# One weight, two transfers: 16 partitions first, then 112

## The chip, the cores and the metric

The kernel runs on one core of one Trainium2 chip. The time is device microseconds of one execution; the number given for a kernel is the median of several. A profile is one further execution with the hardware profiler on; its times count from the start of its span.

## The reference

One decode step of a transformer block with adaptive layer norm, four sequences, width 512, everything in fp32:

```python
mod = (silu(c) @ w_mod).reshape(4, 6, 1, -1)            # c 4x512, w_mod 512x3072
sa, ca, ga, sb, cb, gb = (mod[:, i] for i in range(6))
h = layernorm(x) * (1 + ca) + sa
q = (h @ wq).reshape(4, 1, 32, 128).transpose(0, 2, 1, 3)   # wq 512x4096
p = softmax(q @ k_cache^T * 128**-0.5)                  # k_cache 4x32x4096x128
x = x + ga * ((p @ v_cache) merged over heads @ wo)     # v_cache as k_cache, wo 4096x512
h = layernorm(x) * (1 + cb) + sb
x = x + gb * (silu(h @ w1) @ w2)                        # w1 512x1792, w2 1792x512
```

The two caches are 268 MB each; everything else together is some 30 MB. With one query per sequence each cache element is used once.

## The kernel before, in words

The kernel is first recorded as a list of operations (the class Flow), with each operation's reads and writes by region. Flow works out from these which operation must wait for which, gives every transfer that someone waits for a semaphore of its own, and then emits the operations engine by engine in recorded order. All transfers are issued from SP (nc.sync), in one queue, in the order of the text.

SBUF holds three large slots of 64 KB per partition (ring, slots 0 to 2). Attention runs over 32 blocks n, each of four heads of one sequence: load_k and load_v (both through L374) bring one 8.4 MB block of K or V, 64 KB to each of 128 partitions. VectorE and GpSimd multiply K by the query (L568, GpSimd 40 of the 128 rows of a partition and VectorE 88), VectorE sums (L573), ScalarE takes the exponential (L587), and TensorE multiplies by V (L604). A block's load waits until the slot's former content has been used; K blocks alternate between slots 1 and 2, V blocks use slot 0 (the last one slot 1).

Before the blocks stands the front, which the change touches. Slot 0 holds the modulation weight w_mod there: 128 partitions with four of its rows each, which are one contiguous run of 48 KB per partition (wmv, wmt). Behind it in slot 0 lie the small tensors cg and x0, into which the condition c and the input x go as 16 rows of 512 bytes, to every eighth partition (SB = 8). Slot 2 holds the query weight wq, 64 KB per partition. SP issues, in this order: w_mod (L403), c (L404), x (L405), wq (L408), the first K block (L374). While these arrive, the vector and GpSimd engines build small constant masks. Then silu(c) is taken on ScalarE and VectorE (L466, L467), transposed (L470), multiplied by w_mod on TensorE (L483, sixteen products of it for the first two of the six modulations, 32 for the other four), spread (L491, L495) and copied out (L497); the first layer norm follows, and the query product with wq (L532, L540, then L559 and L563 for each block's query). The second K block goes into slot 2 and the first V block into slot 0, so each waits for the products that read wq or w_mod and the small tensors.

Behind the blocks come the output weight wo in four pieces and w1 and w2 in six (fetch, L366), the output projection (L650), the second layer norm, the feed-forward products (L725, L737), and the store of 16 rows of 512 bytes (L743).

Of the kernel before, what the change touches and what calls it, by code (L numbers as in the profile page):

```python
# [273 lines left out]
def adaln_attention_ffn_kernel(  # L274
# [12 lines left out]
    P = 128  # L287
# [94 lines left out]
    wmv = wm.rearrange("(p k) n -> p k n", p=P)  # L382
# [7 lines left out]
    wmt = s0.take(NK, 6 * D)  # L390
# [9 lines left out]
    xg = const.tile([P, P], F32, name="xg")  # L400
    nc.vector.memset(cg, 0.0)
    nc.gpsimd.memset(x0, 0.0)
    nc.sync.dma_start(wmt, wmv)  # L403
    nc.sync.dma_start(cg[::SB], c)  # L404
    nc.sync.dma_start(x0[::SB], x)  # L405
    s1 = Slot(2)
# [365 lines left out]
```

## Time and profile before

| what | value |
|---|---|
| median of 3 runs | 1316.1 us (1316.02 to 1316.14) |
| the profiled execution's own time | 1316.18 us |
| its span, first to last instruction | 1314.8 us |
| mean granted TensorE clock | 0.647 |
| read from HBM | 567.30 MB |
| busy: VectorE / GpSimd / TensorE / ScalarE | 975.6 / 393.6 / 367.4 / 64.7 us |

How to read the lines that follow: a row of the timeline is start, duration, engine, line of the kernel, operation, what is written and read, the count, and in brackets how long the engine stood idle before and what ended that. PEld is TensorE's weight load, SPq the queue of SP from which transfers are issued. A row of the transfers is target and source, the issuing queue, the count, the size, and the microseconds from issue to landing. A row of the stretches is from:to and length, the busy time of each engine with its number of instructions, the granted TensorE clock, the share of 16 DMA engines in use, and GB/s.

### The profile page before, as it was taken

Reading aid. Unit: us, or ns where it says so; the run is one execution under the profiler, and the core shown is the slowest. Engines: PE = TensorE matmul, PEld = TensorE weight load, DVE = VectorE, ACT = ScalarE, POOL = GpSimd, SP = SyncE. Lnnn points to the kernel's source line nnn. Section 1 sums busy time; section 2 is a strip of 40 time slices with the busy share of each in tenths; the row PEclk is TensorE's granted clock in tenths of the full one; section 3 lists DMA queues with packets and bytes.
Section 4 is the critical chain, followed back from the end, with each engine's and each line's share of the span. In section 5 each row is a group of like instructions: output and inputs, shape, how many; then the busy total and the mean of one; then the engine's idle time right before and its main releaser. Section 6 shows DMA issues by size and latency. Waiting matters only on the chain.

```text
span 1314.8 us, 6115 instructions
## 1 busy us (share of the span) xinstructions
PE 367.4 (28%) x2590; PEld 114.2 (9%) x2590; DVE 975.6 (74%) x256; ACT 64.7 (5%) x198; POOL 393.6 (30%) x106
## 2 busy tenths in 40 slices
PE   3302233211332321133232123323112332311257
PEld 1100101000010100001010000101000010000112
DVE  2399777977777887777788777779777778977762
ACT  1100000000000000000000000000000000000001
POOL 0244312333321333332133333123333212333300
PEclk9756666656666655666665566665566666556669
DMA  9999999999999999999999999999999999999998
GB/s 415 437 423 447 419 441 439 427 441 423 441 439 427 441 433 431 445 421 443 435 429 443 423 441 437 427 441 431 433 443 423 441 435 429 445 423 441 437 423 360
DMA packets 11050, 567.42 MB, mean 432 GB/s; under 512 B 1264, under 2 KB 1312, under 8 KB 1824
## 3 DMA queue, kind: packets, MB, share of 16 engines
q1 hardware_dynamic: 11040, 567.31, 99.7%
q8 instruction: 4, 0.07, 0.0%
q14 instruction: 6, 0.05, 0.0%
HBM read 567.30 MB, written 0.01 MB: 431 GB/s over the span
## 4 chain that ended last, share of the span: by engine, by line
DMA 60%; DVE 38%; PE 1%; another core or an unknown queue 1%; SPq 0%; issue 0%; ACT 0%; DVEq 0%; ACTq 0%
DMA slot<-in_A_k_cache_dram 54%; DVE sc L573 22%; DVE slot L568 15%; DMA slot<-in_B_w_dram 3%; DMA slot<-in_A_wq_dram 3%; PE q L532 1%; PE po L737 0%; DVE rm L577 0%; PE q L540 0%; SPq L366 0%; DVE tr L581 0%; SPq L405 0%; PE q L559 0%; ACT o L557 0%
## 5 line engine op out<-in xcount | busy, mean ns | idle before, releaser
L568 DVE TENSOR_TENSOR slot<-slot,q 128x11264 f32<-128x11264 f32 x32 | 380.4, 11887 | 259.8 <-DMA slot<-in_A_k_cache_dram 259.8
L573 DVE TENSOR_REDUCE sc<-slot 128x88 f32<-128x11264 f32 x64 | 552.9, 8680 | 1.1
L604 PE MATMUL po<-slot,pz 128*32 128x512 f32 x2048 | 294.6, 740 | 901.7 <-PEq L260 836.9
L568 POOL TENSOR_TENSOR slot<-slot,qw 128x5120 f32<-128x5120 f32 x32 | 353.5, 11046 | 220.7 <-DMA slot<-in_A_k_cache_dram 220.7
L589 POOL TENSOR_TENSOR pz<-sc,hm 128x256 f32<-128x256 f32 x64 | 38.1, 617 | 637.9 <-ACT sc L587 637.9
L604 PEld LDWEIGHTS po<-slot,pz 128*32 128x32 f32 x2048 | 80.8, 133 | 1096.6 <-issue 1088.7
L563 ACT ACTIVATE qw<-q 128x128 f32<-128x128 f32 x32 | 8.9, 278 | 562.7 <-DMA slot<-in_A_v_cache_dram 403.4
L557 ACT ACTIVATE o<-qn,sel 128x128 f32<-128x128 f32 x32 | 11.1, 394 | 377.3 <-DMA slot<-in_A_v_cache_dram 377.2
L617 PE MATMUL od<-pc,sg 128*64 128x128 f32 x128 | 17.0, 276 | 12.8 <-PEq L260 12.8
L639 DVE TENSOR_TENSOR o<-og,ra 128x512 f32<-128x512 f32 x2 | 1.4, 692 | 21.2 <-ACT og L620 21.2
L614 ACT ACTIVATE pc<-po 128x512 f32<-128x512 f32 x16 | 9.6, 597 | 151.7 <-PE po L604 151.7
L587 ACT ACTIVATE sc<-sc,nm 128x128 f32<-128x128 f32 x32 | 12.8, 399 | 72.9 <-DVE nm L583 72.6
L617 PEld LDWEIGHTS od<-pc,sg 128*64 128x64 f32 x128 | 13.5, 136 | 26.8 <-issue 26.8
L483 PE MATMUL q<-slot 128*32 128x512 f32 x48 | 9.0, 676 | 19.4 <-DVE slot L470 19.4
L559 PE MATMUL q<-o,blk 128*128 128x256 f32 x32 | 11.2, 431 | 1.5 <-ACT o L557 1.5
L467 DVE SCALAR_TENSOR_TENSOR slot<-slot 128x128 f32<-128x128 f32 x1 | 0.3, 292 | 13.6 <-ACT slot L466 13.6
L491 DVE TENSOR_TENSOR slot<-q,hm 64x256 f32<-64x256 f32 (+1 forms) x8 | 4.1, 548 | 8.2 <-PE q L483 7.3
L577 DVE TENSOR_REDUCE rm<-sc 128x1 f32<-128x128 f32 x32 | 9.1, 286 | 1.1
L650 PE MATMUL acc<-slot,oo 128*4 128x512 f32 x64 | 8.9, 709 | 3.3 <-DVE oo L642 2.5
L620 ACT ACTIVATE og<-od 32x128 f32<-32x128 f32 x32 | 8.5, 267 | 24.3 <-PE od L617 24.1
L549 DVE COPY qn<-q 32x128 f32<-32x128 f32 x2 | 0.6, 284 | 11.1 <-PE q L540 11.0
L581 DVE STREAM_TRANSPOSE tr<-rm 128x32 f32<-128x32 f32 x32 | 6.8, 212 | 1.1
(85 smaller groups left out, 90.8 us busy)
## 6 DMA issues: line engine op xcount, KB each, us to landing
slot<-in_w_mod_dram SPq DMA_DIRECT2D x1, 6144.0 KB, 17.2
slot<-in_A_wo_dram SPq DMA_DIRECT2D x1, 4096.0 KB, 22.2
slot<-in_B_w_dram SPq DMA_DIRECT2D x1, 2688.0 KB, 34.1
slot<-in_A_wo_dram SPq DMA_DIRECT2D x1, 2304.0 KB, 25.2
slot<-in_A_wo_dram SPq DMA_DIRECT2D x1, 1536.0 KB, 27.9
slot<-in_B_w_dram SPq DMA_DIRECT2D x1, 1536.0 KB, 39.0
slot<-in_B_w_dram SPq DMA_DIRECT2D x1, 1280.0 KB, 41.5
slot<-in_B_w_dram SPq DMA_DIRECT2D x1, 896.0 KB, 35.8
```

The costliest lines, as they stand in the source:

```text
L483: nc.tensor.matmul(p[W * u : W * (u + 1), :], csT[:, k, :], wmt[:, k, (i + u) * D : (i + u + 1) * D], start=k == 0, stop=k == NK - 1,)
L532: nc.tensor.matmul(pq[i][W * g : W * (g + 1), :], hT[:, k, :], wqt[:, k, ch * CW : (ch + 1) * CW], start=k == 0, stop=k == NK - 1,)
L557: nc.scalar.activation(m[:, b, :], qn, AF.Copy, scale=sel[:, n + b : n + b + 1])
L559: nc.tensor.matmul(p, blk.rearrange("p i x -> p (i x)"), m, start=True, stop=True)
L568: eng.tensor_mul(kt[n][:, lo:hi, :], kt[n][:, lo:hi, :], src[n].unsqueeze(1).to_broadcast([P, hi - lo, Dh]))
L573: nc.vector.tensor_reduce(sc[n][:, lo:hi], kt[n][:, lo:hi, :], axis=AX.X, op=ALU.add)
L577: nc.vector.tensor_reduce(nm[n], sc[n], axis=AX.X, op=ALU.min)
L587: nc.scalar.activation(sc[n], sc[n], AF.Exp, bias=nm[n], scale=-1.0, accum_out=rs[i][:, c : c + 1])
L589: nc.gpsimd.tensor_mul(pz[h][:, : HG * W].rearrange("p (g x) -> p g x", g=HG)[:, :, E:].rearrange("p g (i j) -> p g i j", i=HP), sc[n][:, ...
L604: nc.tensor.matmul(po[u][W * g : W * (g + 1), :], pz[h][:, o : o + W], vt[n][:, JJ * j : JJ * (j + 1), :].rearrange("p j d -> p (j d)"), s ...
L614: nc.scalar.activation(m, po[u].rearrange("p (j d) -> p j d", j=JJ), AF.Copy)
L617: nc.tensor.matmul(p[: 2 * W], sg[:, j, :], m[:, j, :], start=j == 0, stop=j == JJ - 1)
```

## The change

The load of the modulation weight is issued as two transfers in place of one: partitions 0 to 15 (P // 8 = 16), then partitions 16 to 127. Both write the same places as before, from the same places in memory, 48 KB contiguous per partition: 0.79 MB and 5.51 MB. Each has a semaphore of its own, and the first product that reads the weight waits for both. The order of all other transfers stays.

```diff
     nc.vector.memset(cg, 0.0)
     nc.gpsimd.memset(x0, 0.0)
-    nc.sync.dma_start(wmt, wmv)
+    for lo, hi in ((0, P // 8), (P // 8, P)):
+        nc.sync.dma_start(wmt[lo:hi], wmv[lo:hi])
     nc.sync.dma_start(cg[::SB], c)
     nc.sync.dma_start(x0[::SB], x)
     s1 = Slot(2)
```

## The prediction

> **What bounds the kernel now.** I read the head of the page and its third part first, because they say at once whether any engine has room.
>
> ```profile
> span 1314.8 us, 6115 instructions
> PE 367.4 (28%) x2590; PEld 114.2 (9%) x2590; DVE 975.6 (74%) x256; ACT 64.7 (5%) x198; POOL 393.6 (30%) x106
> DMA packets 11050, 567.42 MB, mean 432 GB/s; under 512 B 1264, under 2 KB 1312, under 8 KB 1824
> q1 hardware_dynamic: 11040, 567.31, 99.7%
> DMA 60%; DVE 38%; PE 1%; another core or an unknown queue 1%; SPq 0%; issue 0%; ACT 0%; DVEq 0%; ACTq 0%
> ```
>
> No computing engine is busy for more than 74% of the span, but the packets of the one load queue fill 99.7% of what 16 DMA engines have. The last line, the chain that ended last, gives VectorE 38%. That share misleads: the chain steps through VectorE where a buffer is handed back, while the transfers run on. Whether they do run on is a question for the stretches of the span.
>
> ```profile
> core 0: us, PE busy (x) PEld busy (x) DVE busy (x) ACT busy (x) POOL busy (x), PEclk, DMA share, GB/s
> 0.00:2.00 2.00, 0.00 (x0) 0.00 (x0) 0.66 (x5) 1.26 (x1) 1.40 (x9) 1.00 0.68 197
> 2.00:18.00 16.00, 0.00 (x0) 0.00 (x0) 2.81 (x14) 0.02 (x1) 0.40 (x1) 1.00 1.02 435
> 18.00:37.30 19.30, 14.84 (x68) 3.94 (x68) 6.73 (x18) 3.08 (x9) 0.29 (x1) 1.00 1.00 435
> 37.30:58.10 20.80, 9.69 (x70) 2.94 (x70) 1.05 (x3) 2.70 (x7) 0.00 (x0) 0.81 0.95 410
> 58.10:1310.00 1251.90, 340.54 (x2388) 105.80 (x2388) 963.77 (x215) 57.67 (x181) 391.53 (x96) 0.63 1.00 434
> 1310.00:1314.80 4.80, 2.33 (x64) 1.56 (x64) 0.58 (x2) 0.00 (x0) 0.00 (x0) 1.00 0.09 35
> ```
>
> The next to last column is the DMA share (a packet counts in the stretch where it starts, hence 1.02). From 2 us to 1310 us it is 1.00 but for 0.95 in one stretch of 20.8 us, that is about 1.0 us not used. There is no idle time of the transfers in which a delay could disappear, and none that an earlier start would fall into. So the time is one stream of bytes with a head of some 2 us and a tail of under 5 us: what the weight's transfer loses or wins at the front arrives at the end.
>
> Last, the front itself: issues in order of time, and the time from issue to landing.
>
> ```profile
> 0.74 0.39 SPq L403 DMA_DIRECT2D slot<-in_w_mod_dram  x1
> 1.19 0.60 SPq L404 DMA_DIRECT2D slot<-in_c_dram  x1
> 1.83 0.83 SPq L405 DMA_DIRECT2D slot<-in_A_x_dram  x1
> 2.70 0.58 SPq L408 DMA_DIRECT2D slot<-in_A_wq_dram  x1
> 18.16 0.31 ACT L466 ACTIVATE slot<-slot 128x128 f32<-128x128 f32 x1 [16.14 <-DMA slot<-in_c_dram]
> 19.38 5.40 PE L483 MATMUL q<-slot 128*32 128x512 f32 x16 [19.38 <-DVE slot L470]
> 36.45 0.79 ACT L497 ACTIVATE mod<-q 128x128 f32<-128x128 f32 x4 [7.03 <-PE q L495]
> 37.33 7.08 PE L532 MATMUL q<-slot 128*32 128x512 f32 x64 [0.92 <-DMA slot<-in_A_wq_dram]
> ```
>
> ```profile
> slot<-in_w_mod_dram SPq DMA_DIRECT2D x1, 6144.0 KB, 17.2
> slot<-in_c_dram SPq DMA_DIRECT2D x1, 8.0 KB, 17.0
> out_dram<-slot SPq DMA_DIRECT2D x1, 8.0 KB, 1.7
> ```
>
> The weight lands at 0.74 + 17.2 = 17.94 us, the condition c right behind it (18.16 us), and the query weight at 37.3 us, back to back.
>
> **How a transfer is laid on the 16 engines.** All transfers are issued from SP; their number is needed, and these rows and those above give it.
>
> ```profile
> slot<-in_A_k_cache_dram SPq DMA_DIRECT2D x32, 48.0
> slot<-in_A_v_cache_dram SPq DMA_DIRECT2D x32, 29.2
> 1262.77 4.22 SPq L366 DMA_DIRECT2D slot<-in_A_wo_dram  x4
> 1267.03 15.07 SPq L366 DMA_DIRECT2D slot<-in_B_w_dram  x6
> ```
>
> 64 + 4 + 6 and the five single ones (weight, c, x, query weight, output) are 79. The page counts 1264 packets under 512 B, and 1264 = 79 x 16: one closing packet for each engine and transfer. So the three transfers of 16 rows also ended on 16 engines each. From 512 B to 2 KB there are 1312 - 1264 = 48 packets, 3 x 16 rows of 512 B: a row travels whole, as one packet. The change therefore very likely does what its words say: 16 rows of 48 KB, one per engine, then 7 per engine, where before it was 8 per engine.
>
> One row of 48 KB (49,152 B) takes an engine 0.997 x 16 x 1314.8 us x 49,152 / 567.31 MB = **1.82 us**. Eight are 14.54 us.
>
> **The change part by part.**
>
> *The head.* The slowest engine landed at 17.94 us, so its eight rows began in effect at 17.94 - 14.54 = 3.40 us, 2.66 us after the issue. The output, 16 rows of 512 B, has landed everywhere 1.7 us after its issue. A first transfer of 16 rows can thus have all engines moving by 0.74 + 1.7 = 2.44 us: a gain of at most 0.96 us, at least nothing (the first rows may be slow for another reason than the number of rows announced). I take 0.96, since the output is the only row here of a 16-row transfer with nothing ahead of it.
>
> *The issue.* One more issue on SP costs 0.39 to 0.60 us there by the rows at L403 and L404. Behind it stand the issues of c, x, the query weight and the first K block; each comes that much later and none is missed, because their packets queue behind 14.5 us of rows anyway. The second part is issued some 0.45 us after the first, before any engine is through its 1.82 us row. The extra 16 closing packets are below what this view resolves. Cost: nothing; without that cover, 0.6 us.
>
> *The wait.* The first product (L483) waits for one transfer more. PE is held there until 19.38 us by VectorE's transpose of silu(c), and c is queued behind both parts of the weight, so the new wait ends first. Nothing else stands behind it on PE but the modulation products themselves.
>
> *The rows.* This is the term that decides. In every large transfer of this trace the 16 engines serve 128 rows, and they run at 434 GB/s for 1250 us, never in each other's way. 16 streams that never meet, on 128 partitions, mean that if the way into the memory is narrow, there are 16 ways of 8 partitions each and each engine keeps to its own. The first part of the change writes only partitions 0 to 15, all 16 engines at once. With g of its rows in one way it takes g x 1.82 us. No transfer here shows g (the 16 rows of c and x lie 8 partitions apart and are tiny). The bounds: g = 1, the engine itself is the limit or neighbours never share, and the change costs nothing here; g = 8, a way is a block of 8 neighbours. Between 2 and 8 I take the geometric middle, **g = 4**: 4 x 1.82 = 7.27 us for 0.79 MB that cost 1.82 us before.
>
> While this lasts the other ways stand idle, and each still has 8 rows to come. The second part is then not 7 but at least 8 x 1.82 = 14.54 us. So for any g above 1 the loss is the whole first part: g x 1.82 us. If the 7 rows of an engine straddle two ways, engines meet now and then in the second part as well: between nothing and one row (1.82 us) more. I take half, 0.91.
>
> [...]
>
> *Sum.* -0.96 (head) + 7.27 (first part, after which the second takes as long as the whole did) + 0.91 = **+7.2 us**. On the profiled execution's own 1316.18 us (span 1314.8 and 1.4 around it; the median of the runs is 1316.1, the same to 0.1) that gives **1323.4 us**.
>
> *Does it arrive at the end?* c, the query weight and the first K block queue behind the weight and slide as it does. If the modulation chain slid further than the query weight (they end within 0.1 us of each other, 37.24 and 37.3), the next cover is the first K block:
>
> ```profile
> 48.51 0.28 ACT L563 ACTIVATE qw<-q 128x128 f32<-128x128 f32 x1 [0.79 <-PE q L559]
> 58.13 11.89 DVE L568 TENSOR_TENSOR slot<-slot,q 128x11264 f32<-128x11264 f32 x1 [10.61 <-DMA slot<-in_A_k_cache_dram]
> 46.34 0.33 SPq L374 DMA_DIRECT2D slot<-in_A_v_cache_dram  x1
> 1310.04 2.33 PE L737 MATMUL po<-slot 128*32 128x128 f32 x64 [0.84 <-DMA slot<-in_B_w_dram]
> ```
>
> The query is ready at 48.8 us and its K block comes at 58.1, 9.3 us of cover; the V block that reuses this slot is issued at 46.3, nearly 12 us ahead of need. The last row shows the end waiting for the last weight's transfer, so a late stream is a late end.
>
> **The rivals.**
>
> *Engines don't meet (g = 1).* Against my forecast: each engine's rate, 27 GB/s, may be the engine's own limit and not that of a way, and the trace would look exactly as it does. Then only the head counts: 0 to -0.96 us, **1315.2 to 1316.2 us**, not slower. It decides if the first 16 rows are in within about 1.82 + 0.96 + 2.6 = 5.4 us of movement.
>
> *Another width.* With g = 2 the sum is 3.63 - 0.96, **1318.9 us**; with g = 8 it is 14.54 - 0.96, **1329.8 us**. Same signs in the trace, other sizes.
>
> *Rounds of neighbours.* If the second part also deals 16 neighbouring partitions at a time, all eight rounds cost 7.27 us: 58.2 - 14.5 = +43.6, **about 1359 us**. Against it: the 128-row loads run undisturbed, so their dealing isn't of this kind.
>
> *The delay is absorbed.* Something would have to make up 5 us in the stream; the rows show 1.0 us unused. **Within 2 us of 1316.1.**
>
> **How the numbers follow.** Forecast (g = 4) 0.68; g = 2 0.06; g = 8 0.06; engines don't meet 0.15; rounds 0.03; absorbed 0.02. The range runs from 1318.8 (g = 2) to 1329.8 (g = 8), which holds 0.80 and leaves out the last three. A difference under 0.2% (2.6 us) can't be told from none here. Slower: 0.68 + 0.06 + 0.06 + 0.03 = 0.83. Same: 0.14 of the case without meeting, and the absorbed one, 0.16. Faster: 0.01, if the head gives far more than its bound.
>
> **What would show it.** The DMA rate between about 2.4 and 9.7 us near 108 GB/s instead of 435, the second part landing near 25 us instead of 17.94, c right behind it, the query weight near 44.5 and the first K block near 65; from there all rows shifted alike, the DMA share 1.00 and the durations of the instructions unchanged. If the weight still lands by 18 us, the step on the rows is wrong and the time is 1316. If it lands at 25 us and the end doesn't move, the reading of the stream is wrong.

## The result

The changed kernel takes **1331.1 us** (median of 4 runs, 1330.95 to 1331.81) against 1316.1: a ratio of 1.0114 (95% interval 1.0102 to 1.0126), or 15.0 us more. Slower was forecast, but by 7.2 us, and the time lies above the range. The head of the page, its third part and the transfer rows of the changed kernel, and the two issues of the weight as the timeline has them in one row:

```profile
span 1329.7 us, 6116 instructions
DMA packets 11066, 567.42 MB, mean 427 GB/s; under 512 B 1280, under 2 KB 1328, under 8 KB 1840
q1 hardware_dynamic: 11056, 567.31, 99.7%
slot<-in_w_mod_dram SPq DMA_DIRECT2D x1, 5376.0 KB, 32.7
slot<-in_w_mod_dram SPq DMA_DIRECT2D x1, 768.0 KB, 10.1
slot<-in_c_dram SPq DMA_DIRECT2D x1, 8.0 KB, 32.5
0.73 0.86 SPq L404 DMA_DIRECT2D slot<-in_w_mod_dram  x2
```

There are 16 packets more, all of them under 512 B: one closing packet per engine for one more transfer, and not one row more. The change is carried out as its words say. The queue is as "busy" as before, 99.7%, for 15 us longer: a share of busy time doesn't show that packets have become slow. The first issue begins at 0.73 us and the second some 0.45 us later (together they take 0.86 us), so the first part lands at about 10.8 us and the second at about 33.9 us. Before, the whole weight had landed at 17.94 us.

The stretches of the changed kernel, then its instructions in order of time:

```profile
0.00:2.00 2.00, 0.00 (x0) 0.00 (x0) 0.66 (x5) 1.27 (x1) 1.40 (x9) 1.00 2.03 270
2.00:9.40 7.40, 0.00 (x0) 0.00 (x0) 2.81 (x14) 0.01 (x1) 0.40 (x1) 1.00 0.85 139
9.40:34.00 24.60, 0.00 (x0) 0.00 (x0) 0.00 (x0) 0.00 (x0) 0.00 (x0) 1.00 0.92 235
34.00:53.10 19.10, 15.58 (x68) 4.01 (x68) 6.73 (x18) 2.30 (x5) 0.29 (x1) 1.00 1.01 439
53.10:73.10 20.00, 9.69 (x70) 2.94 (x70) 1.05 (x3) 3.49 (x11) 0.00 (x0) 0.86 0.98 424
73.10:1325.00 1251.90, 339.98 (x2392) 105.67 (x2396) 963.76 (x215) 57.52 (x181) 391.47 (x96) 0.63 1.00 434
```

```profile
34.13 0.31 ACT L467 ACTIVATE slot<-slot 128x128 f32<-128x128 f32 x1 [32.12 <-DMA slot<-in_c_dram]
35.31 6.13 PE L484 MATMUL q<-slot 128*32 128x512 f32 x16 [35.31 <-DVE slot L471]
53.26 7.07 PE L533 MATMUL q<-slot 128*32 128x512 f32 x64 [0.19 <-DMA slot<-in_A_wq_dram]
73.16 11.89 DVE L569 TENSOR_TENSOR slot<-slot,q 128x11264 f32<-128x11264 f32 x1 [9.71 <-DMA slot<-in_A_k_cache_dram]
```

Everything happened in the first 34 us. While the weight arrives, the core moves 139 and then 235 GB/s in place of 435 (a packet counts in the stretch where it starts, so 11 of the first part's 16 rows stand in the stretch from 0 to 2 us); from 34 us on it is at full rate again, and the 1251.9 us of the blocks move at 434 GB/s, as before. silu(c) starts 15.97 us later than before (34.13 against 18.16), the query product 15.93 (53.26 against 37.33), the first K block's product 15.03 (73.16 against 58.13), and the end comes 14.9 later. About 0.9 us came back in the stretch of the first K block, which used 0.95 of the engines before and uses 0.98 now; why was not tried. All else arrived at the end, as the stream has no slack.

The first part, 0.79 MB, behaves much as forecast: by the packet records of the trace its 16 rows run from 1.78 to 9.01 us, 7.23 us where 7.27 were expected. The second, 5.5 MB, lands 23 us after the first, where at least 14.5 and most likely 15.4 were expected.

### The profile page after: what moved, and what is told of

Same layout as the page of the kernel before. It is cut to its first block, busy times and chain, and to the rows that moved or that the text cites. A ratio compares the mean times of both kernels' runs of the same rounds, so it can differ in the third digit from the quotient of the medians.

```text
span 1329.7 us, 6116 instructions
## 1 busy us (share of the span) xinstructions
PE 367.4 (28%) x2590; PEld 114.1 (9%) x2590; DVE 975.6 (73%) x256; ACT 64.6 (5%) x198; POOL 393.6 (30%) x106
## 3 DMA queue, kind: packets, MB, share of 16 engines
q1 hardware_dynamic: 11056, 567.31, 99.7%
## 4 chain that ended last, share of the span: by engine, by line
DMA 59%; DVE 38%; PE 2%; another core or an unknown queue 1%; issue 0%; ACT 0%; SPq 0%; POOL 0%; DVEq 0%; ACTq 0%; POOLq 0%
DMA slot<-in_A_k_cache_dram 53%; DVE sc L574 22%; DVE slot L569 15%; DMA slot<-in_B_w_dram 3%; DMA slot<-in_c_dram 2%; PE q L484 1%; PE q L533 1%; PE q L496 0%; PE po L738 0%; DVE slot L492 0%; DVE rm L578 0%; PE q L541 0%; DVE tr L582 0%; SPq L366 0%
```

## The experiments

Most runs leave the weight's transfer as it was and put one extra transfer of 48 KB rows ahead of it. It goes into the slot of the first K block, where nobody reads it and the K block later overwrites it, so all computation is that of the kernel before. Since the stream of transfers sets the time, what such a transfer costs is seen in the time of the kernel. The K block's issue then waits until the extra transfer has landed (27.5 us in the run with 112 rows, where it is 3.3 before); the query weight ahead of it lands only at 61.2 us there, so the stream doesn't run dry. The three runs with 16 rows read the same rows of memory, and so do the five with 64, so what differs between them is where they write. The edit, of which only the target differs from run to run:

```diff
+    probe = Slot(1).take(NK, 6 * D)
+    nc.sync.dma_start(probe[TARGET], wmv[:ROWS])
     nc.sync.dma_start(wmt, wmv)
```

Two readings stand against each other. By the prediction's the place decides: g rows in one way take g x 1.82 us. By theory **N** any transfer with fewer than 128 rows is slow, wherever it writes. And where engines meet, either each loses only where it meets another itself, or all 16 go at the pace of those that meet; the trace of before doesn't tell which.

**Sixteen rows, three spacings.** Targets 32:93:4, 0:121:8 and 0:16.

> The kernel before, with one extra transfer ahead of the modulation weight: 16 rows of 48 KB into the slot that the first K block takes later, to partitions 32, 36, ... 92, every fourth. Nobody reads them. [...] Theory N (any transfer with fewer than 128 rows is slow, wherever it writes): +7.2 us, as the first part of the change is said to have cost.

> The same extra transfer to partitions 0, 8, ... 120, every eighth. [...] Theory N: +7.2 us.

> The same extra transfer to partitions 0 to 15, as the first part of the change has it. [...] Theory N: +7.2 us. If only the second part of the change were slow, +1.8 us.

Measured: 1318.4 us (+2.3), 1319.8 us (+3.7; median of eight, of which one took 1334.8) and 1323.0 us (+6.9, ratio 1.0052, 1.0035 to 1.0068), beside 1316.1 before. The landing of the extra transfer in the same order, one row from each kernel's list of transfers:

```profile
slot<-in_w_mod_dram SPq DMA_DIRECT2D x1, 768.0 KB, 4.9
```

```profile
slot<-in_w_mod_dram SPq DMA_DIRECT2D x1, 768.0 KB, 6.7
```

```profile
slot<-in_w_mod_dram SPq DMA_DIRECT2D x1, 768.0 KB, 10.0
```

The same bytes: 1.8 us more to every eighth partition than to every fourth of 32 to 92, and 5.1 us more to the block of 0 to 15. That is once and nearly three times 1.82 us, the time of one row; N, by which all three cost the same, falls. The rest to three times is in the start: by the packet records the spread rows begin at 2.12 us in both kernels and the block at 1.76, so from its first packet the block takes 5.46 us more than the first transfer, 3 x 1.82. Four row times, the forecast's guess, is what the block of 16 shows. And the spread rows cost 2.3 us, not the 0.9 that one row time less the forecast's gain at the head (1.82 - 0.96) gives. Of the 0.5 us over their row time, 0.35 us is that later start (2.12 against 1.77 before); the block doesn't have it. A gain at the head from announcing 16 rows first is not to be seen in either.

**The 112 rows alone.** Target 16:128.

> The kernel before, with an extra transfer of 112 rows of 48 KB to partitions 16 to 127 of the slot of the first K block, ahead of the whole modulation weight: the second part of the change without the first. [...] Engines never in each other's way: 7 x 1.82 = +12.7 us. The second part slow only because the first had set the engines out of step: +12.7 to +14.5 us.

Measured: 1338.4 us, **+22.3** (ratio 1.0168, 1.0151 to 1.0185). The second part is slow by itself; no first part is needed to set the engines out of step. With the 16 rows' 6.9 it also gives the change: 6.9 + 22.3 - 14.5 (the 128 rows that are no longer there) = 14.7, measured 15.0. The 22.3 us lie 9.6 us above seven rows of 1.82 us (12.7).

**Two transfers, cut the other way.**

```diff
-    nc.sync.dma_start(wmt, wmv)
+    fetch(wmt, wmv, 0, 1, NK)
```

Here fetch issues one transfer for the first of a partition's four rows of the weight and one for the other three.

> The weight in two transfers as in the change, but cut along the contiguous run and not along the partitions: all 128 partitions with 12 KB each, then all 128 with 36 KB each. [...] If two transfers in place of one are what costs: +15 us.

Measured: 1316.4 us, ratio 1.0001 (0.9991 to 1.0011). Two transfers in place of one cost nothing that can be told, if both go to all 128 partitions.

**Sixty-four rows, in the middle and below.** Targets 32:96 and 0:64.

> The kernel before, with an extra transfer of 64 rows of 48 KB to partitions 32 to 95 of the slot of the first K block, ahead of the modulation weight. [...] If a transfer with fewer than 128 rows were slow for its number of rows: +14.5 us. If neighbouring rows were dealt to neighbouring engines: 4 x 7.3 = +29 us.

> The same 64 rows to partitions 0 to 63. [...]

Measured: 1323.6 us (+7.4) and 1331.3 us (+15.0). Equal bytes, equal numbers of rows and engines, and the cost doubles with the place. The stretch from 2 to 9 us, which is within the extra transfer in both, of the first and of the second:

```profile
2.00:9.00 7.00, 0.00 (x0) 0.00 (x0) 2.80 (x14) 0.01 (x1) 0.40 (x1) 1.00 1.12 442
```

```profile
2.00:9.00 7.00, 0.00 (x0) 0.00 (x0) 2.81 (x14) 0.01 (x1) 0.40 (x1) 1.00 1.08 232
```

442 against 232 GB/s (the DMA share is over 1 in both, since a packet counts where it starts). So a transfer to half the partitions can run at full rate (435 GB/s before, with all 128), and it depends on the place whether it does. The two runs also bear on how rows are dealt. Dealt one by one, each round would lie on 16 neighbours; at the four row times of partitions 0 to 15 that is an estimated +29 us, and neither run is near it. That an engine gets a run of neighbouring rows instead, four here, is the author's reading; the packet records name no partition. Nor are engines left idle at 0 to 63: the share there is over 1.

**Runs of seven, laid out by hand.** The 112 rows as seven transfers of 16, each with one row per engine:

```diff
+    probe = Slot(1).take(NK, 6 * D)
+    for j in range(7):
+        nc.sync.dma_start(probe[16 + j : 122 + j : 7], wmv[:16])
     nc.sync.dma_start(wmt, wmv)
```

> The 112 rows to partitions 16 to 127 once more, but as seven transfers of 16 rows, the j-th to partitions 16 + j, 23 + j, ... 121 + j: one row per engine, laid out by hand as runs of 7 would be dealt. If one transfer of 112 rows deals runs of 7, this costs the same, +22 us (23 to 26 with the closings of six more transfers). [...]

Measured: 1353.9 us, +37.6, more than was expected. The list of transfers says why:

```profile
slot<-in_w_mod_dram SPq DMA_DIRECT2D x7, 768.0 KB, 5.7
0.73 34.91 SPq L405 DMA_DIRECT2D slot<-in_w_mod_dram  x7
```

Seven transfers, each landed 5.7 us after its issue, and seven issues spread over 34.9 us: they ran one after the other. Flow compares first and last partition only, took the interleaved rows for overlapping, and let SP wait for each. The run says nothing about dealing; in the next one Flow looks at the step between partitions as well:

```diff
+        self.every = step // pitch if n > 1 else 1
...
+        if self.every == other.every and (self.p0 - other.p0) % self.every:
+            return False
```

> The seven transfers of 16 rows once more, but no longer one after the other: in the run before, the recorder took their interleaved partitions for overlapping and held SP until each had landed. Now they are issued back to back. Runs of 7 in step: +22 us as the one transfer of 112 rows (up to 26 with six more closings). [...]

Measured: 1339.2 us, **+23.2**, beside +22.3 for the one transfer of 112 rows; the 0.9 between them was not looked into. All seven are now issued within 4.6 us. The rates from 5 to 13 us, first of the one transfer, then of the seven:

```profile
5.00:9.00 4.00, 0.00 (x0) 0.00 (x0) 0.00 (x0) 0.00 (x0) 0.00 (x0) 1.00 1.25 319
9.00:13.00 4.00, 0.00 (x0) 0.00 (x0) 0.00 (x0) 0.00 (x0) 0.00 (x0) 1.00 0.90 233
```

```profile
5.00:9.00 4.00, 0.00 (x0) 0.00 (x0) 0.00 (x0) 0.00 (x0) 0.00 (x0) 1.00 0.86 209
9.00:13.00 4.00, 0.00 (x0) 0.00 (x0) 0.00 (x0) 0.00 (x0) 0.00 (x0) 1.00 1.00 258
```

These are not alike, 276 against 234 GB/s in the 8 us, but such short stretches depend on which rows happen to start in them. The packet records are the better measure: the median duration in ns, over the 16 engines, of an engine's first to seventh row, and below them the same for the second part of the change.

```
one transfer            3417 3509 2562 3007 3376 3464 3273
seven transfers         2657 3492 2964 3049 3401 3478 3336
second part of change   4334 3518 2480 2952 3442 3512 3278
```

But for the first row, where the seven are still being issued and the change's first part is still under way, and the third, the three agree within 4%. So the one transfer of 112 rows goes as runs of seven do, and the second part of the change goes as the 112 rows do alone. From the second to the seventh row no engine of the change has a row under 2.28 us, where a row of the weight before took 1.82: all 16 engines are slowed, not a few of them.

**Sixty-four rows, moved down in steps.** Between 32:96 and 0:64 the cost doubles. Three targets lie between them: 28:92, 24:88 and 16:80, which are four, eight and sixteen partitions below 32:96.

> The kernel before, with an extra transfer of 64 rows to partitions 28 to 91, four lower than in the run on partitions 32 to 95 that cost +7.4 us. [...]

> [...]

> [...]

| target | cost, us | GB/s from 2 to 9 us | extra transfer, issue to landing, us |
|---|---|---|---|
| 32:96 | +7.4 | 442 | 10.5 |
| 28:92 | +17.2 | 421 | 20.8 |
| 24:88 | +14.9 | 253 | 18.4 |
| 16:80 | +14.9 | 239 | 18.3 |
| 0:64 | +15.0 | 232 | 18.2 |

Two stretches of 28:92, then of 24:88:

```profile
2.00:9.00 7.00, 0.00 (x0) 0.00 (x0) 2.81 (x14) 0.01 (x1) 0.41 (x1) 1.00 1.15 421
9.00:16.00 7.00, 0.00 (x0) 0.00 (x0) 0.00 (x0) 0.00 (x0) 0.00 (x0) 1.00 1.04 302
```

```profile
2.00:9.00 7.00, 0.00 (x0) 0.00 (x0) 2.80 (x14) 0.01 (x1) 0.40 (x1) 1.00 1.15 253
9.00:16.00 7.00, 0.00 (x0) 0.00 (x0) 0.00 (x0) 0.00 (x0) 0.00 (x0) 1.00 0.96 197
```

The single packets say it most plainly. These are the durations in ns of the second row of each of the 16 engines, from the packet records of the traces, in the order of their start:

```
28:92   1815 1815 1815 1815 1815 1815 1815 1815 1815 1815 1815 1815 3622 1815 1815 3631
24:88   3827 3827 3828 3839 3841 3841 3851 3851 3852 3851 3855 3845 3853 3844 3840 3858
```

At 28:92 two of the 16 rows take twice the time, 3.62 and 3.63 us, and the other 14 lose nothing at 1.815: there only those two pay. At 24:88, four partitions lower, all 16 go at one pace, 3.83 to 3.86 us. Further down it gets no worse (+14.9 us at 16:80, +15.0 at 0:64). The extra transfer to 24:88 landed 2.4 us before that to 28:92, and the run with 28:92 is the dearest, +17.2 us. From 2 to 9 us the core moves 421 GB/s there, 2.9 MB where the extra transfer has 3.1, and yet that transfer lands only 20.8 us after its issue: most engines are by then in the weight's own transfer. In that the packet records have rows of 4.1 to 6.2 us, and all the others slow down as well, to some 2.2 to 2.8 us, with 302 GB/s from 9 to 16 us. Which rows hold up which there no record shows.

## Why the prediction was wrong

*The reading of the stream* held. A front that is 15.97 us late gave an end that is 14.9 us late; no computing engine came into it. *The issue* and *the wait* held as far as the runs show: two transfers that go to all 128 partitions each cost the same as one (1316.4 against 1316.2 us), and TensorE still starts behind the transposed silu(c) (35.31 us, released by VectorE).

*The head* gave nothing. A gain of 0.96 us was taken from the output's 1.7 us. By the packet records the 16 engines begin their first rows between 1.77 and 2.90 us before the change and between 1.78 and 3.01 us with it, so announcing 16 rows first starts them no earlier. The page of before had no row for 16 large rows; the lower bound, no gain, was the better choice.

*The first part* held in size: four row times, 7.27 us forecast and 7.23 from its first packet to its last; with the head, +6.3 us forecast and +6.9 measured as an extra transfer. The number four had been a middle between two bounds, which the trace of before could not narrow; as far as that trace goes it was luck. The 7.23 us now show it for partitions 0 to 15; that the place of the rows decides, the three spacings show (4.9, 6.7 and 10.0 us to land).

*The second part* is the step that failed. The prediction says that it takes at least 8 x 1.82 = 14.54 us and adds "between nothing and one row (1.82 us) more. I take half, 0.91". Alone it cost 22.3 us, 6.8 more than those 15.45. Two things were missing in that bound. It let an engine lose one row in all, but by the packet records the medians of the seven rows of the 112 are 2.6 to 3.5 us, 22.6 us together, an estimate near the 22.3 measured; seven rows of 1.82 are 12.7. And the sum counted the delay of the engines that meet, each for itself, while at 24:88 all 16 were held up at once (3.83 to 3.86 us for the second row). Which of the 112 rows hold up which isn't shown, so the 22.3 us is measured and not derived.

With the measured terms the sum comes out: 6.9 + 22.3 - 14.5 = +14.7 us.

*The range* ended at 1329.8, with eight rows to a way. That bound covers the first part's unknown only; the unknown of the second part had a bound of one row and should have gone up to what two engines to a way throughout give by the prediction's own reading, an estimated 7 x 2 x 1.82 = 25.5 us, which with the first part makes 1334.

*The rivals.* Engines that don't meet, and a delay that is absorbed, are excluded by the runs with 16 rows and by the end of the trace. Rounds of neighbours (+43.6) are excluded by the 64 rows in the middle (+7.4). Other widths (3.63 or 14.54 us for the first part) are excluded by its 7.23 us. The time alone would have pointed to eight rows to a way (1329.8 forecast, 1331.1 measured); only the rows of the first part tell that the loss lies in the second.

What stays open: why all 16 engines are slow at 24:88 and only two at 28:92, why a row of the 112 takes neither 1.82 nor 3.84 us but 2.5 to 3.5, and the 0.9 us that came back at the first K block.

## What to carry to other kernels

Cut a large transfer along its contiguous runs and not along the partitions: here the one cost nothing (1316.4 against 1316.2 us), the other 15.0 us. If it must be part of the partitions, measure the place it writes to, because 64 rows cost 7.4 us at partitions 32 to 95 and 15.0 us at 0 to 63. In a kernel that lives off one stream of transfers a slow front goes straight to the end (15.97 us late at the front, 14.9 at the end here), and a busy share of 99.7%, the same before and after, hides it: look at GB/s by stretch. Where a term of a sum rests on engines that "now and then" meet, take its upper bound from all of them waiting, not from the one that is in the way.

## What was not expected of the hardware

Of 64 rows to partitions 24 to 87 the second row took all 16 engines some 3.84 us, while four partitions higher it took two of them 3.6 us and the other 14 kept to 1.815. After that, at partitions 28 to 91, the rest slowed down as well, to some 2.2 to 2.8 us. And 64 partitions suffice for the full rate if they are 32 to 95: from the second row on 1.82 us a row on all 16 engines, as with 128 partitions.
